# Rows of six experts gathered by quarters of their channels, with a pause of GpSimd behind each tile, and turned by VectorE in squares, in an attention and top-1 mixture-of-experts kernel

## The chip, the cores and the metric

The kernel runs on one core of a Trainium2 chip. Its time is the device time of one execution in microseconds (us). A profile is one execution taken by the hardware profiler; its span is the time from the first to the last instruction seen. The engines are TensorE (PE: matrix products, weight loads shown apart as PEld), VectorE (DVE), ScalarE (ACT), GpSimd (POOL) and SyncE (SP). In this kernel SP issues the plain DMA transfers and POOL the indirect ones, which gather or scatter rows by a list of row numbers.

## The reference

Everything is float32. An attention with 4 batches, 8 heads, 768 positions and 64 channels a head makes a matrix `x` of 3072 tokens by 512 channels. A router sends each token to one of 8 experts, and each expert has two layers.

```python
# attention: a key is seen if it is global (pos < 8) or local (0 <= rel < 96)
scores = q @ k.T / sqrt(D) + bias_of_head_and_distance     # unseen keys: -1e6
attn_out = softmax(scores) @ v
x = attn_out.transpose(0, 2, 1, 3).reshape(3072, 512)
# router
xn, en = x / (norm(x) + 1e-6), expert_emb / (norm(expert_emb) + 1e-6)
logits = xn @ en.T / tau
expert_idx, gate_w = argmax(logits, 1), max(softmax(logits), 1)
# experts: w1 [8, 512, 1024], w2 [8, 1024, 512]
for e in range(8):
    mask = expert_idx == e
    h = maximum(x[mask] @ w1[e], 0)
    out[mask] = gate_w[mask, None] * (h @ w2[e])
```

## The kernel before, in words

**Stages.** The attention and the router come first and take some 200 us. Each token's row of `x` is written to DRAM (`x_dram`), and the list of tokens of each expert is built there. Then the eight experts follow one after the other. In the profile expert 0 stands before 234 us; the first products of experts 1 to 7 begin on PE at 234.2, 268.5, 320.8, 353.6, 390.5, 429.6 and 479.0 us, and the span ends at 522.0. Only experts 2 to 7 are gathered otherwise by the change.

**One expert.** An expert has up to 512 slots, in four tiles of 128 rows. How many of them are computed is read at run time (a `Switch` with one arm for each width, 256 to 512 in steps of 32 from expert 1 on). Its work is:

1. *Gathering* (`gather_rows`, L1000). POOL issues four indirect DMAs, one for each tile; each brings 128 rows of 2 KB to 128 partitions (`xg`, 256 KB). The buffers of `xg` are eight, two experts' worth.
2. *Turning* (`turn_row`). The products need channels on the partitions, tokens along the rows. PE transposes each tile in four pieces of 128x128 (L1026) into PSUM, ACT copies the result in two halves to `xT` (L1029). This is done for expert e+1 while PE works on expert e: one tile behind each of the products 1 to 4 of the first layer (`between`).
3. *First layer* (`first_by_seven`, L1312). The product of `xT` and `w1` is cut in 2x2 blocks and computed with seven block products instead of eight. For this DVE makes sums and differences of the blocks ahead of time: of the tokens (`token_sums`, L1054 to L1057), and of the weights (`first_sums`, L1079 to L1082). DVE adds the products (L1324), ACT takes the relu (L1326, L1343), and the hidden rows lie in `hT`. PSUM has four banks (`big`) for these products.
4. *Second layer.* The tiles from the third on, and the remaining part tile of 64 or 32 rows, are plain products (L1245, L1258) that ACT writes to `y_arm` and `y_part`. The first two tiles are computed as a `Pair`, again with seven products (L1117), whose first is called m. Its results are two tiles `y0` and `y1`, from a pool `yp` of four buffers, so that expert e writes into the buffers of expert e-2. Half of `y0` is written by ACT in `fourth` (L1164); its other half by DVE (L1129) in a function `rest`, which is run after the next expert's first layer.
5. *Scattering* (`scatter_rows`, L1264). POOL issues indirect DMAs that put the rows in the output: two tiles of `y_arm`, two parts, `y0` of the expert before, `y1` of this one; six for each expert, called S(e) here. The first set has seven.

**What sets the order.** A manual schedule: each engine executes its instructions in the order in which the program names them, and semaphores hold an instruction until its data are there. The main loop runs over e = 0 to 7. In each round `prepare(e+1)` issues the four gathers of the next expert, called G(e+1) here; then come the pending scatters S(e-1); then SP is given the loads of `w1` and `w2` of expert e+1; then POOL a `drain` (L1754); then `expert(e)`. So POOL's order is G(0), G(1), drain, G(2), S(0), drain, G(3), S(1), drain, and so on.

**Weights.** `load_weights` issues one DMA of 2 MB for `w1` (L167) and one of 2 MB for `w2` (L168) on SP's queue. Two sets of buffers alternate. The load of expert e+1 waits for product m of expert e-1's pair (`k.out_again`), and that of expert 2 for the last scatter of S(0). The partition p of `w1` holds the channels p, 128 + p, 256 + p and 384 + p.

**Spare time of DVE.** `first_by_seven` and `Pair.begin` take lists of small functions (`spare`). At fixed places between the products they run one list (`fill`), which puts sums for later products into DVE's order there.

Of the kernel before, what the change touches and what calls it, by code (L numbers as in the profile page):

```python
# [9 lines left out]
F32 = mybir.dt.float32  # L10
# [10 lines left out]
P = 128  # L21
# [2 lines left out]
PIECES = 32  # L24
FIRST = 256
LACE = 16
WIDTHS = [128] + list(range(160, CAP + 1, 32))
PAIR = WIDTHS.index(256)

# [134 lines left out]

def load_weights(k, e, w):
    nc = k.nc
    first = nc.sync.dma_start(w[0][:], k.w1[e].rearrange("(c p) f -> p c f", p=P))  # L167
    nc.sync.dma_start(w[1][:], k.w2[e].rearrange("(f p) m -> p f m", p=P))  # L168
    return first

# [824 lines left out]
def gather_rows(k, ids, xgp, NJ=CAP // P, upto=None):  # L995

    xgs, issued = [], []
    for j in range(NJ):
        xg = xgp.tile([P, k.DM], F32, name="xg", tag="xg")
        i = k.nc.gpsimd.indirect_dma_start(  # L1000
            out=xg[:], out_offset=None, in_=k.x_dram[0 : upto or k.N + 1, :],
            in_offset=bass.IndirectOffsetOnAxis(ap=ids[:, j, 0:1], axis=0),
        )
        xgs.append(xg)
        issued.append(i.ins)
    return xgs, issued


def new_turned(k):
    return k.xtp.tile([P, k.NC, 2, CAP // 2], F32, name="xT", tag="xT")  # L1010

# [280 lines left out]
            between(f)  # L1292


def first_by_seven(k, now, hT, w, between, spare):


    nc, h = k.nc, w // 2
    a = first_weights(k, now.w[0])
    b = [[now.xT[:, 2 * i : 2 * i + 2, j] for j in range(2)] for i in range(2)]  # L1300
    s1, s2, s3, s4 = now.first_sums
    t1, t2, t3, t4 = now.token_sums
    out = [[laced(hT[:, 4 * i : 4 * i + 4, 0:w])[:, j] for j in range(2)] for i in range(2)]
    number = [0]

    def banks():
        return [k.big.tile([P, CAP], F32, name="big", tag="big") for _ in range(2)]

    def product(to, x, y, add=False):
        for f in range(4):  # L1310
            for l in range(2):
                nc.tensor.matmul(to[f // 2][:, f % 2 * 256 : f % 2 * 256 + h], lhsT=x[:, l, f * P : (f + 1) * P], rhs=y[:, l, 0:h],  # L1312
                                 start=not (add or f % 2 or l), stop=True, skip_group_check=True)
        between(number[0])
        number[0] += 1

    def pairs(ps, q):
        for i in range(2):
            x = ps[i][:].rearrange("p (f n) -> p f n", f=2)[:, :, 0:h].rearrange("p f (q i) -> p f q i", i=LACE)
            yield x, q[:, 2 * i : 2 * i + 2]  # L1320

    def plus(ps, z, q, last=False):
        for (x, to), (_, z) in zip(pairs(ps, q), pairs(ps, z)):
            nc.vector.tensor_tensor(out=to, in0=x, in1=z, op=ALU.add)  # L1324
            if last:
                nc.scalar.activation(to, to, AF.Relu)  # L1326
        fill()

    def fill():
        for make in spare.pop(0):  # L1330
            make()

    (q11, q12), (q21, q22) = out
    fill()
    x, y = banks(), banks()
    product(x, a[0][0], b[0][0])
    for ps, q in pairs(x, q21):
        nc.scalar.copy(out=q, in_=ps)
    product(y, s2, t2)
    plus(y, q21, q12)  # L1340
    product(x, a[0][1], b[1][0], True)
    for ps, q in pairs(x, q11):
        nc.scalar.activation(q, ps, AF.Relu)  # L1343
    product(y, s3, t3, True)
    plus(y, q21, q22)
    v = banks()
    product(v, s1, t1)
    plus(v, q22, q22, True)
    product(y, a[1][1], t4, True)
    plus(y, q21, q21, True)  # L1350
    product(v, s4, b[1][1], True)
    plus(v, q12, q12, True)


def expert(k, now, coming, widths, unfinished):


    tc = k.tc
    w1, w2 = now.w
    hT = new_hidden(k)  # L1360
    if coming:
        coming.xT = new_turned(k)

    def between(f):
        at = {1: (0,), 2: (1,), 3: (2,), 4: (3,)} if now.e else {5: (0,), 6: (1, 2), 7: (3,)}
        for j in at.get(f, ()) if coming else ():
            turn_row(k, coming.rows, coming.xT, j, k.nc.scalar.copy)

    a = [[hT[:, 4 * j : 4 * j + 4, i * P : (i + 1) * P] for j in range(2)] for i in range(2)]
    now.sums, spare = weight_sums(k, w2)  # L1370
    left, making = hidden_sums(k, a)
    more, ahead = [], []
    if coming:
        coming.token_sums, more = token_sums(k, coming.xT)
        if now.e:
            coming.first_sums, ahead = first_sums(k, coming.w[0])
    spare = [spare[:2], spare[2:], ahead[:1], ahead[1:2], more[:2], []]
    if now.e == 1:
        spare[2:6] = [], ahead[:1], ahead[1:2] + more[:1], more[1:2]
    tiles = range(2 if now.e else 1, CAP // P)  # L1380
    ps = None if now.e else k.work0.tile([P, k.DM], F32, name="work", tag="work")
    k.order = list(range(4, 8)) + list(range(4)) if now.e else list(range(8))
    steps = widths_of(now.e)
    for arm in tc.Switch(now.width.index, len(steps), hint=now.width.hint):
        w = steps[arm]
        if now.e:
            first_by_seven(k, now, hT, w, between, list(spare))
            for make in making:
                make()
        else:  # L1390
            first_by_eight(k, now.xT, w1, hT, w, between)
        for size in (32, 64):
            if w % (2 * size) >= size:
                part_in_arm(k, now, hT, w2, w // (2 * size) * 2 * size, size)
        for j in tiles:
            if j < w // P:
                second_in_arm(k, now, hT, w2, j)
        if ps:
            second(k, ps, hT, w2, range(k.NF // 2))

    def scatters():
        for j in tiles:
            scatter_rows(k, now.y[:, j - 1, :], now.tile_ids[:, j : j + 1])
        for size in (64, 32):
            scatter_rows(k, now.y_part[size][:], now.parts[size][0], P // size)

    def choose_next():
        if coming:
            give_hint(k, coming.e, widths[coming.e])

    out = [scatters]
    if now.e:
        pair = Pair(k, now.rows, a, left, w2, now.sums, not coming)
        choose_next()
        out += unfinished.pop()()
        number = [lambda: widths.append(take_width(k, now.e + 2))] if now.e + 2 < k.E else []
        if now.e == k.E - 2:
            number.append(lambda: load_flag(k))
        if now.e == 2:
            ahead.append(lambda: flag_leftover(k))  # L1420
        pair.begin(spare=(more[2:], number + ahead[2:3], ahead[3:]))
        ps = k.work0.tile([P, k.DM], F32, name="work", tag="work")
        unfinished.append(pair.end(ps[:, 0:256]))
        out.append(pair.scatter(1))
    else:
        choose_next()
        widths.append(take_width(k, 2))
        out += unfinished.pop()()
        for make in more:
            make()  # L1430
        second(k, ps, hT, w2, range(k.NF // 2, k.NF))
        unfinished.append(lambda: end_second(k, now.rows, ps))
    return out
# [172 lines left out]
def kernel(  # L1606
# [40 lines left out]
    with ExitStack() as moe:  # L1647
# [43 lines left out]
        def prepare(e):  # L1691
            t = Net()
            t.e = e
            t.y, t.y_part = ys[e % 2]
            xgs, t.gathers = gather_rows(n, n.ids[:, e], n.xgp)
            t.rows = n.mt[:, e], n.ids[:, e], xgs
            if e < 2:
                t.w = n.w[e]
            else:
                t.w = new_weights(n, (wp_a, n.wp_b)[e % 2])  # L1700
            return t

        with tc.manual_schedule(engines=ORDERED | set(ARMS) | {mybir.EngineType.Pool}):
# [26 lines left out]
            for j in range(CAP // P):  # L1730
                turn_row(n, coming.rows, coming.xT, j, nc.vector.tensor_copy)
            cast(2, n.E)
            split_rows(n, n.mt)
            for y, parts in ys:
                for x in (y, *parts.values()):
# [5 lines left out]
            for e in range(n.E):  # L1741
                now, coming = coming, None
                parts_of(n, now)
                now.width = widths[e]
                if e == 1:
                    now.first_sums = first
                if e + 1 < n.E:
                    coming = prepare(e + 1)
                for scatter in pending:
                    scatter()  # L1750
                if e and coming:
                    wait_for(n, load_weights(n, e + 1, coming.w), [n.outs[-1] if e == 1 else n.out_again])

                nc.gpsimd.drain()  # L1754
                pending = expert(n, now, coming, widths, unfinished)
# [33 lines left out]
```

## Time and profile before

| | |
|---|---|
| time, median of 3 runs | 520.47 us (517.8 to 521.45) |
| profiled execution | 523.85 us, its span 522.0 us |
| busy in the span: PE, DVE, ACT, POOL | 500.9, 301.3, 197.4, 148.7 us |
| lengths of experts 1 to 7 on PE | 34.3, 52.3, 32.8, 36.9, 39.1, 49.4, 43.0 us |
| PE busy in them | 33.0, 52.2, 32.8, 36.6, 39.1, 49.4, 37.6 us |
| DVE busy in them | 22.0, 23.3, 21.4, 21.9, 22.2, 23.2, 16.2 us |
| POOL busy in them | 11.6, 10.6, 11.2, 11.3, 10.9, 6.7, 6.9 us |
| first gather of G(2) to G(7) starts at | 215.8, 238.2, 270.2, 323.9, 356.4, 393.3 us |
| product m of experts 1 to 7 starts at | 254.9, 308.3, 341.5, 377.7, 417.3, 466.7, 504.1 us |
| issue of w1 for experts 2 to 7 | 236.9, 256.9, 310.4, 343.5, 380.3, 419.4 us |

A line of instructions gives the start, the duration, the engine, the line of the code, the operation, what it writes and reads, and in brackets how long the engine had been idle before it and which instruction ended that. A line of the chain gives the start, the duration and what ran. A line of windows gives the stretch, its length, the busy time of PE, PEld, DVE, ACT and POOL with the number of instructions, the granted clock of PE, the mean busy share of the DMA engines, and GB/s.

### The profile page before, as it was taken

To read this page: it belongs to the slowest core of one execution; us is meant where nothing else is said; L and a number is where in the kernel's file an instruction comes from. 1 tells how busy PE (TensorE), PEld (TensorE's weight loads), DVE (VectorE), ACT (ScalarE), POOL (GpSimd) and SP (SyncE) were. 2 spreads that over 40 slices of the span, in tenths; PEclk is the share of its full clock that TensorE was granted. 3 is DMA by queue.
4 is the path that set the end of the run, shared out by engine and by line. 5 is a ranking of instruction groups with operands and counts; after the bars stand their busy time and mean duration, and the time that the engine had idled before them with its cause. 6 is when DMAs were issued, how large, how long until landed. Compare 5 with 4: busy or idle time off the path is not lost.

```text
span 522.0 us, 13698 instructions
## 1 busy us (share of the span) xinstructions
PE 500.9 (96%) x5606; PEld 412.8 (79%) x5606; DVE 301.3 (58%) x602; ACT 197.4 (38%) x493; POOL 148.7 (28%) x169
## 2 busy tenths in 40 slices
PE   8999999999987998899989999999999999999995
PEld 7777787787765687859878659989889789859964
DVE  5646667766774664846745606765646644715531
ACT  4966776777644311303222312412312222302210
POOL 4221121432443326253340024153053050013023
PEclk9999999999998999999999999999999999999999
DMA  8989999998524336818682018457066065001001
GB/s 166 202 174 182 220 238 217 222 232 204 131 69 121 104 62 143 251 46 290 207 287 99 2 50 285 156 198 263 3 217 242 4 224 164 1 15 68 0 22 67
DMA packets 111421, 76.32 MB, mean 146 GB/s; under 512 B 87077, under 2 KB 95269, under 8 KB 111281
## 3 DMA queue, kind: packets, MB, share of 16 engines
q1 hardware_dynamic: 102769, 59.00, 42.6%
q0 software_dynamic: 6912, 15.26, 8.7%
q8 instruction: 63, 1.03, 0.9%
q14 instruction: 77, 0.63, 0.5%
q10 hardware_dynamic: 1600, 0.39, 0.3%
HBM read 61.66 MB, written 17.16 MB: 151 GB/s over the span
## 4 chain that ended last, share of the span: by engine, by line
PE 64%; issue 24%; POOL 5%; DVE 3%; ACT 2%; POOLq 1%; DMA 1%; DVEq 0%
PE big L1312 15%; PE big L1117 8%; PE od L512 7%; PE pa L483 6%; PE pa L458 4%; PE work L1258 3%; PE od L522 3%; PE pa L681 3%; PE work L1117 3%; POOL out_dram L1264 3%; PE work L1245 3%; PE work L1026 2%; PE big L1288 2%; PE pa L585 2%; PE work L1036 1%
## 5 line engine op out<-in xcount | busy, mean ns | idle before, releaser
L496 DVE TENSOR_TENSOR ex<-ex,table 126x768 f32<-126x768 f32 x64 | 60.3, 947 | 41.4 <-ACT ex L489 38.5
L1324 DVE TENSOR_TENSOR hT<-big,hT 128x320 f32<-128x320 f32 (+4 forms) x70 | 39.4, 566 | 49.2 <-PE big L1312 46.8
L1264 POOL DMA_INDIRECT out_dram<-y_arm,tids x17 | 17.0, 1002 | 170.4 <-ACT y_arm L1247 121.3
L489 ACT ACTIVATE ex<-pa 126x384 f32<-126x384 f32 (+1 forms) x128 | 53.7, 476 | 24.0 <-PE pa L483 17.7
L1312 PE MATMUL big<-xT,w1t 128*128 128x160 f32 (+4 forms) x336 | 59.4, 330 | 1.3 <-issue 1.3
L1312 PEld LDWEIGHTS big<-xT,w1t 128*128 128x128 f32 x336 | 54.2, 190 | 4.0 <-issue 2.2
L512 PE MATMUL od<-ex,v 126*64 126x192 f32 (+1 forms) x576 | 46.8, 309 | 0.0
L1000 POOL DMA_INDIRECT xg<-x_dram,idss x32 | 32.3, 1011 | 43.9 <-PE big L1312 21.7
L483 PE MATMUL pa<-qT,kT 64*32 64x128 f32 (+3 forms) x2048 | 40.8, 268 | 2.8 <-issue 2.5
L483 PEld LDWEIGHTS pa<-qT,kT 64*32 64x32 f32 (+1 forms) x2048 | 30.5, 107 | 15.2 <-issue 10.6
L512 PEld LDWEIGHTS od<-ex,v 126*64 126x64 f32 x576 | 35.2, 138 | 7.7 <-issue 3.5
L259 POOL DMA_INDIRECT meta<-mt,slot x24 | 27.4, 1141 | 43.8 <-DVE rd L556 17.8
L1312 PE MATMUL big<-xsum,fsum 128*128 128x160 f32 (+4 forms) x224 | 39.6, 330 | 0.0
L1029 ACT COPY xT<-work 128x256 f32<-128x256 f32 x56 | 18.0, 377 | 56.7 <-PE work L1026 55.3
L1312 PEld LDWEIGHTS big<-xsum,fsum 128*128 128x128 f32 x224 | 36.1, 190 | 1.1
L1245 PE MATMUL work<-w2t,hT 128*128 128x512 f32 x80 | 35.1, 593 | 0.0
L1117 PE MATMUL big<-wsum,hsum 128*128 128x256 f32 x136 | 31.1, 380 | 1.5 <-issue 1.0
L1326 ACT ACTIVATE hT<-hT 128x320 f32<-128x320 f32 (+4 forms) x42 | 21.6, 533 | 25.5 <-DVE hT L1324 25.3
L433 POOL COPY v<-v 30x896 f32<-30x896 f32 (+1 forms) x15 | 16.6, 1119 | 49.0 <-DMA v<-in_v_dram 30.5
L1117 PEld LDWEIGHTS big<-wsum,hsum 128*128 128x128 f32 x136 | 25.7, 190 | 6.0 <-issue 1.8
L1245 PEld LDWEIGHTS work<-w2t,hT 128*128 128x128 f32 x80 | 15.1, 190 | 17.7 <-issue 17.6
L1122 DVE TENSOR_TENSOR ptmp<-big,ptmp 128x256 f32<-128x256 f32 x16 | 6.7, 421 | 37.6 <-PE big L1117 16.9
(246 smaller groups left out, 903.0 us busy)
## 6 DMA issues: line engine op xcount, KB each, us to landing
w1t<-in_moe_w_dram SPq DMA_DIRECT2D x6, 2048.0 KB
w2t<-in_moe_w_dram SPq DMA_DIRECT2D x6, 2048.0 KB
v<-in_v_dram SPq DMA_DIRECT2D x32, 192.0 KB
x_dram<-xs SPq DMA_DIRECT2D x23, 256.0 KB
k<-in_k_dram SPq DMA_DIRECT2D x28, 192.0 KB
q<-in_q_dram SPq DMA_DIRECT2D x28, 192.0 KB
w1t<-in_moe_w_dram SPq DMA_DIRECT2D x32, 128.0 KB
w2t<-in_moe_w_dram SPq DMA_DIRECT2D x32, 128.0 KB
```

The costliest lines, as they stand in the source:

```text
L259: i = nc.gpsimd.indirect_dma_start(out=k.meta[:], out_offset=bass.IndirectOffsetOnAxis(ap=slot[:, t : t + 1], axis=0), in_=mt[:, t, :], in ...
L483: i = nc.tensor.matmul(u.sp[e][k0:k1, a * n + c0 : a * n + c1], lhsT=t.kT[rows, j, k0:k1], rhs=t.qT[rows, j * BLK + c0 : j * BLK + c1], st ...
L489: nc.scalar.activation(u.ex[:, e], u.sp[e][0:ROWS, 0 : 2 * u.n].rearrange("p (a c) -> p a c", a=2), AF.Exp, scale=k.scale)
L496: nc.vector.tensor_tensor(out=exv, in0=exv, in1=tab[:, :, 0 : u.n // BLK, :], op=ALU.mult)
L512: nc.tensor.matmul(g.od[a][e * D : (e + 1) * D, at : at + c1 - c0], lhsT=g.v[0:ROWS, 2 * a + e, u.j, :], rhs=u.ex[:, e, a, c0:c1], start=f ...
L1000: i = k.nc.gpsimd.indirect_dma_start(out=xg[:], out_offset=None, in_=k.x_dram[0 : upto or k.N + 1, :], in_offset=bass.IndirectOffsetOnAxis ...
L1117: i = self.k.nc.tensor.matmul(ps, lhsT=x[:, f, :], rhs=w[:, f, :], start=f == 0 and not add, stop=True, skip_group_check=True)
L1245: nc.tensor.matmul(ps[:], lhsT=hT[:, f, j * P : (j + 1) * P], rhs=w2[:, f, :], start=i == 0, stop=i == k.NF - 1)
L1264: i = k.nc.gpsimd.indirect_dma_start(out=k.out.rearrange("t (i m) -> (t i) m", i=n), out_offset=bass.IndirectOffsetOnAxis(ap=ids, axis=0), ...
L1312: nc.tensor.matmul(to[f // 2][:, f % 2 * 256 : f % 2 * 256 + h], lhsT=x[:, l, f * P : (f + 1) * P], rhs=y[:, l, 0:h], start=not (add or f ...
L1324: nc.vector.tensor_tensor(out=to, in0=x, in1=z, op=ALU.add)
L1326: nc.scalar.activation(to, to, AF.Relu)
```

## The change

For experts 2 to 7, the channels of a row are taken as four quarters of 128. A tile of 128 slots is gathered with four indirect DMAs instead of one: DMA g brings, to each of the 128 partitions, a quarter of a row (512 bytes) into columns 128g to 128g + 127 of `xg`. The lists of row numbers (`squares`, made once by 16 small DVE operations) are mixed so that partitions 32b to 32b + 31 of `xg` hold the quarter b of the tokens in slots 32g to 32g + 31. After that, a transposition that only works inside squares of 32x32 is enough to get channels on partitions: one DVE instruction for each tile (`turn_squares`), which writes to `xT` directly. The transposes on PE and the copies on ACT are gone for these experts. The four turns of expert e+1 stand in DVE's order behind `rest` of expert e and ahead of the pair's first addition.

Behind the four gathers of each tile, POOL executes a small copy that reads the first element of each quarter. It waits until all four have landed, and whatever comes later on POOL stands behind it.

In the turned rows, partition 32b + j and group c hold channel 128b + 32c + j. So `w1` has to be loaded in that order, which is done with four DMAs of 32 partitions (512 KB each) instead of one of 128. Expert 0 and 1 keep their gathers, their turning on PE, and weights loaded earlier in small parts.

Expert 2's four tiles are split: two are gathered before S(0), two after it. The sums of tokens of the next expert, of which two stood inside the first layer, now all stand behind the turns. The sums of weights are spread otherwise over the lists in the first layer.

```diff
@@ load_weights
-    first = nc.sync.dma_start(w[0][:], k.w1[e].rearrange("(c p) f -> p c f", p=P))
+    first = [nc.sync.dma_start(w[0][b * SQ : (b + 1) * SQ], k.w1[e, b * P : (b + 1) * P].rearrange("(c j) f -> j c f", j=SQ))
+             for b in range(4)][0]
@@
+def square_rows(k):
+    k.landed = k.tp.tile([P, 4], F32, name="landed")
+    k.squares = k.tp.tile([P, k.E, CAP // P, 4], I32, name="squares")
+    for b in range(4):
+        for g in range(4):
+            k.nc.vector.tensor_scalar(out=k.squares[b * SQ : (b + 1) * SQ, 2:, :, g], in0=k.mt[g * SQ : (g + 1) * SQ, 2:, :, 0],
+                                      scalar1=4.0, scalar2=float(b), op0=ALU.mult, op1=ALU.add)
+
+def gather_quarters(k, ids, xgs, lo, hi):
+    src = k.x_dram[:, :].rearrange("t (b c) -> (t b) c", b=4)
+    for j in range(lo, hi):
+        for g in range(4):
+            k.nc.gpsimd.indirect_dma_start(
+                out=xgs[j][:, g * P : (g + 1) * P], out_offset=None, in_=src,
+                in_offset=bass.IndirectOffsetOnAxis(ap=ids[:, j, g : g + 1], axis=0),
+            )
+        k.nc.gpsimd.tensor_copy(out=k.landed[0:1, :], in_=xgs[j][0:1, ::P])
+
+def turn_squares(k, xgs, xT, j):
+    half = P // 2
+    k.nc.vector.transpose(
+        out=xT[:, :, :, j * half : (j + 1) * half].rearrange("p c a (g i) -> p g c a i", i=LACE),
+        in_=xgs[j][:].rearrange("p (g c r) -> p g c r", g=4, r=SQ),
+    )
@@ first_by_seven, product
-        between(number[0])
-        number[0] += 1
@@ expert
-        at = {1: (0,), 2: (1,), 3: (2,), 4: (3,)} if now.e else {5: (0,), 6: (1, 2), 7: (3,)}
-        for j in at.get(f, ()) if coming else ():
+        for j in {5: (0,), 6: (1, 2), 7: (3,)}.get(f, ()):
             turn_row(k, coming.rows, coming.xT, j, k.nc.scalar.copy)
...
+            turns = [lambda j=j: turn_squares(k, coming.rows[2], coming.xT, j) for j in range(CAP // P)]
-    spare = [spare[:2], spare[2:], ahead[:1], ahead[1:2], more[:2], []]
-    if now.e == 1:
-        spare[2:6] = [], ahead[:1], ahead[1:2] + more[:1], more[1:2]
+    spare = [[], spare[:2], spare[2:3], spare[3:], ahead[:1], ahead[1:2]]
...
-        pair.begin(spare=(more[2:], number + ahead[2:3], ahead[3:]))
+        for make in turns:
+            make()
+        pair.begin(spare=(more, number, ahead[2:]))
@@ prepare
-            xgs, t.gathers = gather_rows(n, n.ids[:, e], n.xgp)
+            if e < 2:
+                xgs, t.gathers = gather_rows(n, n.ids[:, e], n.xgp)
+            else:
+                xgs = [n.xgp.tile([P, n.DM], F32, name="xg", tag="xg") for _ in range(CAP // P)]
+                gather_quarters(n, n.squares[:, e], xgs, 0, 2 if e == 2 else 4)
@@ the main loop
             cast(2, n.E)
+            square_rows(n)
             split_rows(n, n.mt)
...
                 for scatter in pending:
                     scatter()
+                if e == 1:
+                    gather_quarters(n, n.squares[:, 2], coming.rows[2], 2, 4)
                 if e and coming:
                     wait_for(n, load_weights(n, e + 1, coming.w), [n.outs[-1] if e == 1 else n.out_again])
```

More of the change, by code (lines that the diff above doesn't have):

```diff
@@ L26 @@
 LACE = 16
+SQ = 32
 WIDTHS = [128] + list(range(160, CAP + 1, 32))
@@ L1292, in first_by_eight, with first_by_seven @@
             between(f)
-def first_by_seven(k, now, hT, w, between, spare):
+def first_by_seven(k, now, hT, w, spare):
     nc, h = k.nc, w // 2
@@ L1303, in first_by_seven @@
     out = [[laced(hT[:, 4 * i : 4 * i + 4, 0:w])[:, j] for j in range(2)] for i in range(2)]
-    number = [0]
     def banks():
@@ L1371, in expert @@
     left, making = hidden_sums(k, a)
-    more, ahead = [], []
+    more, ahead, turns = [], [], []
     if coming:
@@ L1386, in expert @@
         if now.e:
-            first_by_seven(k, now, hT, w, between, list(spare))
+            first_by_seven(k, now, hT, w, list(spare))
             for make in making:
```

## The prediction

> **What bounds the kernel now.** I read the page's busy row first, then the windows by expert, the chain that ended last, and GpSimd's instructions in order of time.
>
> ```profile
> PE 500.9 (96%) x5606; PEld 412.8 (79%) x5606; DVE 301.3 (58%) x602; ACT 197.4 (38%) x493; POOL 148.7 (28%) x169
> ```
>
> PE is busy 96% of the span. Whether that holds in each expert is told by the windows that run from one expert's first product to the next one's (here experts 2, 4 and 5):
>
> ```profile
> 268.50:320.80 52.30, 52.22 (x218) 39.81 (x219) 23.25 (x35) 12.03 (x25) 10.60 (x10) 1.00 0.34 120
> 353.60:390.50 36.90, 36.61 (x283) 32.97 (x282) 21.86 (x31) 10.17 (x25) 11.33 (x10) 1.00 0.47 164
> 390.50:429.60 39.10, 39.10 (x202) 33.43 (x200) 22.22 (x31) 10.28 (x24) 10.89 (x10) 1.00 0.45 156
> ```
>
> After the length come PE, PEld, DVE, ACT and POOL. PE fills every stretch. DVE works 22 of about 37 us, POOL 11. So what leaves PE's stream shortens the span one for one, as long as nothing else becomes late. The chain shows what the turning costs on PE (inside expert 3):
>
> ```profile
> 320.97 4.35 PE big L1312 x32
> 325.32 0.44 PE work L1026 x4
> 325.76 2.18 PE big L1312 x16
> 327.93 0.44 PE work L1026 x4
> ```
>
> Four transposes take 0.44 us of the chain between two products. Their row of the groups says 273 ns each, but there they overlap one another, so 0.44 is what is saved. Last, POOL around expert 3's product m (341.5):
>
> ```profile
> 342.39 1.02 POOL L1264 DMA_INDIRECT out_dram<-y_arm,tids  x1 [13.27 <-ACT y L1260]
> ...
> 351.62 0.98 POOL L1264 DMA_INDIRECT out_dram<-y,idss  x1 [2.15 <-DVE y L1122]
> 356.44 0.99 POOL L1000 DMA_INDIRECT xg<-x_dram,idss  x1 [3.84 <-PE big L1312]
> ```
>
> Before this block POOL had idled 13 us. The 3.84 us between last scatter and next gather is the drain of L1754. POOL is now 10 us of scatters, 4 of drain, 5 of gathers, and then it waits for work.
>
> [...] the small scatters land 1.9 to 3.1 us after their start with no load beside them, a full 256 KB scatter 3.7 to 4.6. [...] in the trace small scatters beside a w1 load land after 5.1 to 6.7 us, full gathers beside w2 after 4.3 to 4.8, and that of G(3) beside both after 7.5. [...] The 2 MB loads over 128 partitions last 7.0 to 8.6 us here; no run shows a load over 32. [...]
>
> **The change part by part.** G(e) is the gathering for expert e, S(e) the scatters of expert e (six). POOL's order stays G(e+1), S(e-1), drain.
>
> *PE.* 16 transposes less per expert that prepares a later one, six experts: 4 x 0.44 = 1.76, x 6 = **-10.6 us** if nothing is late. ACT's 48 copies (L1029) go, off the path.
>
> *DVE.* Four transposes of 128x512 per expert, priced as the nearest row, a 128x512 tensor_tensor of 0.69 us (bounds 0.3 and 1.2): 2.8 us. They stand between `rest` and u2; the token sums (the same in number) follow them. In all 25 of 37 us: hidden, since the next expert's second product wants the last of these sums several us later. If the cover went, up to 2 us per expert. 16 tiny operations at 210 us, some 0.17 each, 2.7 us, before `split_rows`: expert 0's products cover them (bounds 0 and 1). Weight sums begin a slot later: 0, covered.
>
> *SP.* Three more issues, 0.38 each, per load: w2 is put in the queue 1.1 us later, hidden by its several us of slack. Nothing else waits in that queue. A w1 load in quarters I price at 10 us (bounds 7, as now, and 14[...]). w1 of experts 3 to 7 is issued a pair before it is read: hidden at all of these.
>
> *POOL.* One tile is now four gathers and a copy that waits for all four landings. Starts are 1.3 us apart: 3 x 1.3 = 3.9 until the fourth starts, then its landing, then 0.4 for wake and copy (POOL copies of this size take 0.18). For the landing of the last 64 KB I take 3.0 alone (bounds 2.3[...], and 3.8, a full scatter) and 5.2 beside a load (bounds 4.0 and 6.5). So a tile costs 7.3 alone, 9.5 beside a load. Loads run some 18 of the 42 us of an expert with its stall, 43%: mean 8.25, **G = 33 us instead of 5** (bounds 29 and 36.6). With S, 6 x 1.32 = 7.9, and 3.9 of drain the POOL cycle is 45 us, while e3, e4, e5 need 31.0, 35.1, 37.3 on PE. In that order POOL can't keep up; what remains is its head start, from e2 (50.5 us).
>
> *Who waits for POOL.* Behind the pause stand S(e-1) and the drain. `fourth` of expert e (L1164, ACT) writes the y0 buffer of expert e-2 (yp has four), whose scatter is fifth in S(e-1), now behind all of G(e+1). So the buffer is free 4 x 1.32 = 5.3 + landing 4.4 = 9.7 us after G(e+1) ends. Behind `fourth` waits the bank that the next expert's second product writes in its second half, 3.3 us after that expert begins (1.5 products of 2.18); with 0.4 for the ACT operation, expert e+1 can begin, as if undisturbed, at **end of G(e+1) + 6.8**. The turning alone would ask for less: copy, four turns, +4.6.
>
> *The chain of times.* G(2) begins at 215.8 as before; two tiles, 14.6 -> 230.4. S(0) has seven scatters, 9.2 -> 239.6. Its last starts at 238.3 instead of 233.19; w1(2) is issued 3.75 after that start, as before, at 242.1 instead of 236.94, lands at 252, and DVE's first sum on it is wanted at 248.4: **+3.4 us** net for expert 1. Expert 2 starts at 268.5 + 3.4 - 1.8 = 270.1; e3 at 320.7; on PE alone e4 at 351.7, e5 at 386.8, e6 at 424.1. POOL: two tiles of G(2) beside loads, 19.0 -> 258.6; then drain + G: G(3) 295.5; and each next one 7.9 + 3.9 + 33 = 44.8 later: G(4) 340.3, G(5) 385.1. S finds its results ready in each. Expert 4: 347.1, no stall. Expert 5: 385.1 + 6.8 = 391.9 instead of 386.8, **stall 5.1**. G(6) 429.9, expert 6 at 436.7 instead of 391.9 + 37.3 = 429.2, **stall 7.5**. G(7) 474.7, +6.8 = 481.5; PE has e7 at 436.7 + 47.6 = 484.3: no stall in the wide e6. Then 43.0 as before: 527.3.
> Sum: -10.6 + 3.4 + 5.1 + 7.5 = +5.4 against the span of 522.0. The profiled execution took 523.85, the median of the runs is 520.47; I carry the difference over: 520.47 + 5.4 = 525.9, said as **526 us**.
>
> **The rivals.** *POOL keeps up.* The sum of stalls is 12.6 at G = 33, and four Gs stand in the time of expert 6, so it moves 4 us per us of G: no stall is left at G = 29.8, 7.5 us a tile. Then -10.6 + 3.4 = -7.2: **513 us**. For it: landings of 64 KB alone could be 2.3, and gathers of G(4) to G(7) beside w2 landed after 4.3 to 4.8 even at 256 KB. Against: 512-byte pieces beside a load, and G(3)'s 7.5.
> *POOL deeper.* G = 36.6, a tile of 9.15, as when landings are 3.6 and 6.5: 4 x 3.6 = +14.4 on 526, **540 us**; it also stalls e5 and perhaps e7. For it: small scatters at 5.1 to 6.7 beside w1. It decides from 8.0 us per tile, where the loss outweighs the saving (slower than before from G = 31.7).
> *A draw.* G about 31.7, or the saving eaten by w1(2) alone: quarters of w1 that take 14 us make expert 1 4 us later still with POOL keeping up: **517 to 521 us**.
> That the change doesn't do what it says: the 96 transposes leave PE's program for certain; only the cost is open.
>
> **How the numbers follow.** About 1% is what a measurement of this kernel tells from no change: under 515.3 is faster, over 525.7 slower. POOL-bound near 526: 0.34 (522 to 532). Deeper: 0.23. Keeps up: 0.23. Draw: 0.20. The cell at 526 lies on the edge of "slower"; of its 0.34, 0.09 falls within 1%, and of the draw all but 0.06, which fall to faster and slower alike. Faster 0.26, same 0.23, slower 0.51. Range 512.5 to 541: all of the middle cases and the near part of both ends.
>
> **What would show it.** Right: no L1026 between products in the chain; POOL's list with gaps of 3 to 5 us ahead of each small copy, G of 33 us; POOL full from 240 to 475; PE idle, on ACT's `fourth` (hidden under "y"), at the second product of experts 5 and 6. Wrong: tiles of 7 us or less and every window 1.76 us shorter; w1 quarters that land after 14 us; or DVE transposes of over 1.2 us, with PE waiting for token sums at the second product of every expert; or gathers of 512 bytes that slow the loads they meet, so that w2 or w1 is late.

## The result, and the profile after

The changed kernel takes **560.58 us** (median of 4 runs, 555.28 to 562.41) against 519.67 us for the kernel before, measured beside it: ratio 1.0771, interval 1.0687 to 1.0855. It is slower by 41 us; 526 us were forecast, and the range ended at 541. The profiled execution has a span of 559.4 us against 522.0.

The busy row of the page, after:

```profile
PE 497.6 (89%) x5510; PEld 409.1 (73%) x5510; DVE 317.7 (57%) x642; ACT 183.3 (33%) x445; POOL 234.7 (42%) x265
```

PE has its 96 transposes less (5510 instead of 5606 matrix instructions). But it is no longer busy all the time: 89% instead of 96%. The windows by expert, for experts 2, 4 and 5 (length, PE, PEld, DVE, ACT, POOL, then the granted clock of PE):

```profile
276.40:327.10 50.70, 50.58 (x204) 38.00 (x202) 27.10 (x41) 9.76 (x17) 25.33 (x26) 1.00 0.44 120
369.20:417.80 48.60, 36.74 (x265) 32.42 (x264) 23.76 (x35) 7.79 (x17) 25.29 (x26) 0.92 0.45 124
417.80:467.20 49.40, 41.02 (x186) 34.23 (x185) 24.15 (x35) 7.89 (x16) 24.07 (x27) 0.91 0.45 122
```

Expert 2 keeps what the change promises: 50.7 instead of 52.3 us. Experts 4 and 5 need about 49 us each instead of 36.9 and 39.1, and PE stands idle in them. Experts 1 and 3 lose too: 46.3 instead of 34.3, 42.1 instead of 32.8. Experts 6 and 7 are as before within 0.4 us. Lost are 12.0, 9.3, 11.7 and 10.3 us in experts 1, 3, 4 and 5; 4.1 us come back before expert 1 starts (230.1 instead of 234.2), and 2 in experts 2 and 6. The 4.1 us are not shown to be the change's: in `before_w1_spread` below, which has the old gathers and turns, expert 1 starts at 227.9.

The chain (the work that ended last, followed back) ahead of 418 us, around the end of expert 4, has no PE in it at all (these are the lines of its last tile):

```profile
396.69 0.97 POOL xg L1026
...
397.97 0.95 POOL xg L1026
...
399.22 0.95 POOL xg L1026
...
400.47 8.59 DMA xg<-x_dram,squares
...
409.23 0.15 POOL landed L1030
```

The same tile in POOL's own list, with the tile before it, which has no load beside it:

```profile
388.53 0.97 POOL L1026 DMA_INDIRECT xg<-x_dram,squares  x1 [0.16 <-issue]
...
396.01 0.18 POOL L1030 COPY landed<-xg 1x4 f32<-1x4 f32 x1 [1.83 <-DMA xg<-x_dram,squares]
396.69 0.97 POOL L1026 DMA_INDIRECT xg<-x_dram,squares  x1 [0.50 <-issue]
...
400.47 0.95 POOL L1026 DMA_INDIRECT xg<-x_dram,squares  x1 [0.30 <-issue]
409.21 0.18 POOL L1030 COPY landed<-xg 1x4 f32<-1x4 f32 x1 [7.79 <-DMA xg<-x_dram,squares]
410.02 1.03 POOL L1297 DMA_INDIRECT out_dram<-y_arm,tids  x1 [0.64 <-issue]
...
421.62 0.99 POOL L1026 DMA_INDIRECT xg<-x_dram,squares  x1 [3.66 <-issue]
```

The copy of the quiet tile waits 1.83 us, that of the last tile 7.79: `w1` of expert 6 was issued at 396.46 and its four quarters took until 409.4. After it come six scatters without a wait (their results have long been ready) and the drain of 3.66 us. From G(3) on POOL waits for PE no more; it runs its own round of 48.3, 55.4, 49.0 and 49.0 us (first gather of G(3) to G(7): 268.9, 317.2, 372.6, 421.6, 470.6), and the experts follow it.

How they follow is told by VectorE and PE:

```profile
409.18 0.71 DVE L1036 STREAM_TRANSPOSE xT<-xg 128x512 f32<-128x512 f32 x1 [10.75 <-DMA xg<-x_dram,squares]
409.82 0.39 DVE L1155 TENSOR_TENSOR ptmp<-big,ptmp 128x256 f32<-128x256 f32 x1
410.13 0.67 DVE L1087 TENSOR_TENSOR xsum<-xT 128x512 f32<-128x512 f32 x1
...
412.29 0.69 DVE L1090 TENSOR_TENSOR xsum<-xT,xsum 128x512 f32<-128x512 f32 x1
412.90 0.42 DVE L1155 TENSOR_TENSOR ptmp<-big,ptmp 128x256 f32<-128x256 f32 x1
```

```profile
414.27 3.78 PE L1150 MATMUL work<-w2t,hsum 128*128 128x256 f32 x8 [9.21 <-ACT ptmp L1203]
417.84 4.07 PE L1344 MATMUL big<-xT,w1t 128*128 128x192 f32 x16
```

The fourth turn waits 10.75 us for its tile. Behind it stand the pair's first addition, the four sums of tokens and the pair's second addition; from these ACT makes what it must write before PE may run the last product of the pair (9.21 us of waiting). Expert 5 begins 8.45 us after G(5), the gathering for it, is through (409.39). The same distance is found at the ends of experts 3 and 5 (8.44 and 8.46).

Expert 1 loses its time in another way. `w1` of expert 2 is issued at 245.43, since S(0) stands behind two tiles of G(2), and it takes 11.4 us (in the chain). VectorE's first sum on it stands ahead of additions that expert 1 needs:

```profile
260.74 1.55 PE L1291 MATMUL work<-w2t,hT 128*64 128x256 f32 x6 [13.41 <-ACT hT L1356]
```

### The profile page after: what moved, and what is told of

The parts are those of the page before. It is cut to its first block, busy times and chain, and to the rows that moved or that the text cites. A ratio compares the mean times of both kernels' runs of the same rounds, so it can differ in the third digit from the quotient of the medians.

```text
span 559.4 us, 13682 instructions
## 1 busy us (share of the span) xinstructions
PE 497.6 (89%) x5510; PEld 409.1 (73%) x5510; DVE 317.7 (57%) x642; ACT 183.3 (33%) x445; POOL 234.7 (42%) x265
## 4 chain that ended last, share of the span: by engine, by line
PE 45%; issue 17%; DMA 16%; POOL 14%; DVE 3%; ACT 2%; POOLq 1%; SPq 0%; ACTq 0%; DVEq 0%
DMA xg<-x_dram,squares 11%; PE big L1344 9%; POOL xg L1026 8%; PE od L514 6%; PE pa L485 5%; PE big L1150 4%; PE pa L460 4%; POOL out_dram L1297 3%; PE od L524 3%; PE pa L683 2%; DMA w1t<-in_moe_w_dram 2%; PE work L1291 2%; PE pa L587 2%; PE big L1321 2%; PE work L1150 1%
## 5 line engine op out<-in xcount | busy, mean ns | idle before, releaser
L1026 POOL DMA_INDIRECT xg<-x_dram,squares x96 | 105.6, 1100 | 53.2 <-issue 44.9
L498 DVE TENSOR_TENSOR ex<-ex,table 126x768 f32<-126x768 f32 x64 | 61.8, 974 | 37.6 <-ACT ex L491 37.3
L1354 DVE TENSOR_TENSOR hT<-big,hT 128x320 f32<-128x320 f32 (+4 forms) x70 | 39.2, 565 | 69.2 <-PE big L1344 39.1
L1344 PE MATMUL big<-xT,w1t 128*128 128x160 f32 (+4 forms) x336 | 61.6, 338 | 4.1 <-ACT hT L1368 4.0
L1344 PEld LDWEIGHTS big<-xT,w1t 128*128 128x128 f32 x336 | 56.8, 196 | 8.4 <-ACT hT L1368 4.9
L1030 POOL COPY landed<-xg 1x4 f32<-1x4 f32 x24 | 8.8, 365 | 81.6 <-DMA xg<-x_dram,squares 81.6
L1150 PE MATMUL work<-w2t,hsum 128*128 128x256 f32 x56 | 19.0, 498 | 25.6 <-ACT ptmp L1203 25.6
L514 PEld LDWEIGHTS od<-ex,v 126*64 126x64 f32 x576 | 35.2, 138 | 7.8 <-issue 3.5
L485 PE MATMUL pa<-qT,kT 64*32 64x128 f32 (+3 forms) x2048 | 38.1, 270 | 0.2 <-issue 0.2
L1150 PEld LDWEIGHTS work<-w2t,hsum 128*128 128x128 f32 x56 | 13.5, 250 | 29.6 <-ACT ptmp L1203 27.2
L1291 PE MATMUL work<-w2t,hT 128*32 128x128 f32 (+1 forms) x320 | 22.1, 328 | 13.4 <-ACT hT L1356 13.4
L1036 DVE STREAM_TRANSPOSE xT<-xg 128x512 f32<-128x512 f32 x24 | 15.4, 684 | 30.8 <-DMA xg<-x_dram,squares 30.8
```

The costliest lines, as they stand in the source:

```text
L485: i = nc.tensor.matmul(u.sp[e][k0:k1, a * n + c0 : a * n + c1], lhsT=t.kT[rows, j, k0:k1], rhs=t.qT[rows, j * BLK + c0 : j * BLK + c1], st ...
L498: nc.vector.tensor_tensor(out=exv, in0=exv, in1=tab[:, :, 0 : u.n // BLK, :], op=ALU.mult)
L514: nc.tensor.matmul(g.od[a][e * D : (e + 1) * D, at : at + c1 - c0], lhsT=g.v[0:ROWS, 2 * a + e, u.j, :], rhs=u.ex[:, e, a, c0:c1], start=f ...
L1026: k.nc.gpsimd.indirect_dma_start(out=xgs[j][:, g * P : (g + 1) * P], out_offset=None, in_=src, in_offset=bass.IndirectOffsetOnAxis(ap=ids[ ...
L1150: i = self.k.nc.tensor.matmul(ps, lhsT=x[:, f, :], rhs=w[:, f, :], start=f == 0 and not add, stop=True, skip_group_check=True)
L1291: nc.tensor.matmul(ps[i * size : (i + 1) * size, 0:m], lhsT=hT[:, f, base : base + size], rhs=w2[:, f, i * m : (i + 1) * m], start=o == 0, ...
```

## The experiments

The kernels below were measured on six chips, and this turned out to matter: the kernel before takes 518.6 to 519.1 us on three of them, 520.9 to 524.7 on the three others. So each kernel is compared with the kernel before on its own chip, and the verdict on the pause rests on four kernels measured on one chip, which come first. The texts of what was expected name theories by letters: A holds the pause for the cause, C the loading of `w1` in quarters, G the 4 KB runs of the quarters, F and F1 the chip.

**The pause and the quarters of w1, two by two on one chip.** `no_pause` leaves out the small copy (nothing of the output comes from it). `w1_linear` keeps the pause and lets VectorE read its squares at a stride of four, so that partition p holds channels 4p to 4p + 3, and `w1` is again one DMA to 128 partitions, with runs of 16 KB. The fourth kernel has both edits.

```diff
-        k.nc.gpsimd.tensor_copy(out=k.landed[0:1, :], in_=xgs[j][0:1, ::P])      # no_pause
```
```diff
-    first = [nc.sync.dma_start(w[0][b * SQ : (b + 1) * SQ], k.w1[e, b * P : (b + 1) * P].rearrange("(c j) f -> j c f", j=SQ))
-             for b in range(4)][0]
+    first = nc.sync.dma_start(w[0][:], k.w1[e].rearrange("(p c) f -> p c f", p=P))
...
-        in_=xgs[j][:].rearrange("p (g c r) -> p g c r", g=4, r=SQ),
+        in_=xgs[j][:].rearrange("p (g r c) -> p g c r", g=4, r=SQ),
```

> The changed kernel once more, so that the four kernels of pause or not and w1 in quarters or in one load stand on one chip. Theory F1 (without a pause the chip decides how long PE stands still beside gathers; with it GpSimd's round is the bound on any chip): 552 to 565.

> As no_pause. Theory F1: 555 to 575 on a chip where the kernel before takes 520.5 or more, 515 to 525 where it takes less. Theory C (w1 in quarters by 4 KB runs makes it slow wherever it runs): 555 or more.

> As w1_linear. Theory F1 and theory A (GpSimd's round of 45 us and more is the bound): 540 to 552 on any chip.

> As w1_linear_no_pause. Theory F1: 511 to 516 where the kernel before takes less than 520, 540 or more where it takes more. Theory C: 511 to 516 on any chip.

Measured, beside 518.70 us for the kernel before:

| | w1 in quarters | w1 in one DMA |
|---|---|---|
| with the pause | 557.49 (1.0779, 1.0696 to 1.0863) | 547.80 (1.0566, 1.0469 to 1.0663) |
| without | 517.43 (0.9980, 0.9957 to 1.0003) | 513.69 (0.9902, 0.9872 to 0.9932) |

The pause costs 40 us with the quarters and 34 without (the four runs of the 547.80 lie between 542.7 and 553.4, so rather 30 to 34). The quarters cost 10 us with the pause and 4 without, net of VectorE's slower reading that takes their place (a transposition took 1079 ns in the fourth kernel, 684 in the changed one). So on this chip the pause is the loss, all of it: without the pause the change is level with the kernel before (the interval holds 1), and without the quarters as well it is 1% below it. Theory F1 and theory A give all four cells; theory C falls with `no_pause` at 517. The windows of `no_pause` on this chip, experts 4 and 5:

```profile
350.70:385.90 35.20, 34.80 (x266) 31.27 (x266) 24.77 (x37) 7.90 (x17) 22.08 (x21) 1.00 0.63 166
385.90:424.60 38.70, 37.60 (x185) 31.75 (x184) 24.09 (x35) 8.01 (x16) 24.97 (x26) 1.00 0.61 161
```

PE is full again, in 35.2 and 38.7 us, while POOL does the same gathers. Its list (the first and the last three of one G; the first scatter behind them):

```profile
364.81 1.24 POOL L1026 DMA_INDIRECT xg<-x_dram,squares  x1 [7.33 <-issue]
366.36 0.98 POOL L1026 DMA_INDIRECT xg<-x_dram,squares  x1 [0.30 <-issue]
...
385.18 0.95 POOL L1026 DMA_INDIRECT xg<-x_dram,squares  x1 [0.30 <-issue]
386.44 0.95 POOL L1026 DMA_INDIRECT xg<-x_dram,squares  x1 [0.30 <-issue]
387.69 1.02 POOL L1296 DMA_INDIRECT out_dram<-y_arm,tids  x1 [0.30 <-issue]
```

Sixteen gathers take 22.9 us, not 37. Of the 10.6 us that the transposes took from PE, `no_pause` gives back 4 in expert 1, where PE still waits 5.22 us for the late `w1` (38.2 us instead of 34.3); experts 2 to 6 are 5.6 us shorter in sum, not 8.8. In the kernel with both edits PE waits 2.18 us in expert 1.

**One pause instead of four** (the copy behind the loop over the tiles, on the last tile).

```diff
-        k.nc.gpsimd.tensor_copy(out=k.landed[0:1, :], in_=xgs[j][0:1, ::P])
+    k.nc.gpsimd.tensor_copy(out=k.landed[0:1, :], in_=xgs[hi - 1][0:1, ::P])
```

> w1_linear with one small copy behind all four tiles instead of one behind each. Theory A (a pause costs what the last landing takes, 3 us alone and 5 to 7 beside a load, four times an expert, and GpSimd's round of 45 us is the bound): G 21 + 3 to 6, a round of 36 to 39 us against 31 to 37 on PE; 515 to 523 us. Theory A'' (any wait of GpSimd for a gather holds up the rest): 535 us or more.

514.82 us, 0.9937 (0.9915 to 0.9958). A wait of POOL for a gather is harmless in itself:

```profile
355.48 0.18 POOL L1029 COPY landed<-xg 1x4 f32<-1x4 f32 x1 [5.16 <-DMA xg<-x_dram,squares]
```

It waits 5.16 us here, beside a load, and nobody is late for it: PE has no gap over 1.1 us from there to expert 7. Only the sum of four in a round longer than the expert makes the loss. Theory A holds.

**The turns later.** The fourth kernel of the table, with the turns behind the pair's first addition and the sums of tokens behind its second.

```diff
-        for make in turns:
-            make()
-        pair.begin(spare=(more, number, ahead[2:]))
+        pair.begin(spare=(turns, more + number, ahead[2:]))
```

> w1_linear_no_pause with VectorE's four turns behind the pair's first addition and the four sums of tokens behind its second, instead of both ahead of the pair's first and second. If the gaps of 1 to 2 us on PE inside the pair come from the additions that stand behind 4.3 us of turns, they go: 508 to 512 us. If not (the sums come too late for the next expert's second product): 514 to 520 us.

513.60 us, 0.9906 (0.9869 to 0.9942), against 513.89 and 513.69 for the kernel that it was made from, on other chips. That is no gain that the measurement tells: of the gaps in the pair the one of expert 3 goes, that of expert 1 stays (2.8 us), and one of 1.6 us appears between two products of expert 3's first layer. The expectation of 508 to 512 was a miss.

**A chip that is worse for this.** Four kernels were measured on it: `no_pause`, `w1_linear`'s forerunner `w1_wide` with and without pause, and the kernel before with `w1` in quarters.

> The changed kernel without the small copies behind each tile; quarters, squares and w1 in quarters stay. Theory A (the pause makes GpSimd the bound, a round of G 37 + S 8 + drain 4 = 49 us against 31 to 37 us that an expert needs on PE): sixteen gathers at 1.3 us are 21 us, a round 33 us, PE is the bound again except perhaps in expert 3; w1(2) still comes some 3 us late; 512 to 518 us. Theory B (not the pause, but gathers of 512-byte pieces beside w1 in quarters, which land late, so that VectorE's turns are late anyway): over 540 us, with VectorE idle for some 8 us ahead of a turn.

560.80 us, 1.0740 (1.0667 to 1.0814): taken alone it says the opposite of the table above, that the pause costs nothing. With `before_w1_quarters` below it led to theory C, that the quarters keep everything else waiting.

```diff
-    first = nc.sync.dma_start(w[0][:], k.w1[e].rearrange("(c p) f -> p c f", p=P))
+    first = [nc.sync.dma_start(w[0][b * 32 : (b + 1) * 32], k.w1[e].rearrange("(c p) f -> p c f", p=P)[b * 32 : (b + 1) * 32])
+             for b in range(4)][0]
```

> The kernel before with w1 in four DMAs of 32 partitions each, its own layout kept. Theory A: w1 takes 11.5 to 12 us instead of 7 to 8.6, hidden everywhere but for expert 2, whose first sum wants w1 at 247 us and gets it at 249 to 250: +2 to +4, 522 to 525 us. Theory B (the slow load is a main cost by itself): over 532 us.

> before_w1_quarters once more, on another chip if there is one. Theory F1 (on a chip where the kernel before takes less than 520 a slow load only costs what is late for it): w1(2) lands 3 us late, 520 to 525. Theory C (the quarters keep the next arm's instructions waiting anywhere): 531 to 536.

533.64 us, 1.0247 (1.0175 to 1.0319), and on another chip 538.74, 1.0307 (1.0235 to 1.0380), with the kernel before at 520.91 and 524.65. The quarters take 11.2 to 12.2 us in the first of these traces instead of 7.0 to 8.6. Beyond the late `w1` of expert 2, a second delay is longer than before: PE's jump into the next expert's arm (these lines are of the second trace).

```profile
L1785 PEldq COMPARE_BRANCH  x16: 292/348/7277, 207.7 to 509.4; - x16
```
```profile
274.53 2.04 PE L1313 MATMUL big<-xT,w1t 128*128 128x256 f32 x4 [5.15 <-issue]
```

The longest jump lasts 7.28 us (3.76 in the kernel before); it starts at 266.8 and ends just before expert 2, ahead of which PE idles 5.15 us with nothing that the profile shows as awaited. Both were measured on chips on which the kernel before takes over 520 us, so what the quarters cost the kernel before on the others is not measured; the table's 4 us is the nearest.

The cut over every fourth partition, with the same counts and sizes:

```diff
+    first = [nc.sync.dma_start(w[0][b::4], k.w1[e].rearrange("(c p) f -> p c f", p=P)[b::4])
+             for b in range(4)][0]
```

> The kernel before with w1 in four DMAs of 32 partitions, but every fourth partition (b, b+4, ...) instead of 32 neighbours; counts, sizes and bytes as in before_w1_quarters. Theory C ([...]the load lasts 12 us, and the instructions of the next arm and w1(2) come behind it): loads last 7 to 8.6 us again and the time is that of the kernel before, 519 to 523. Theory D (four DMAs instead of one, or more semaphores and queue work, make it): loads last 11 us or more, 530 to 536.

518.97 us, 1.0007 (0.9993 to 1.0022). Its loads last 7.4 to 9.0 us, and a packet of 4 KB takes 0.16 us, in the quarters of 32 neighbours 0.32. So it is the neighbours that make the load slow, not the number of DMAs: on that, theory C holds (with quarters of neighbours the loads last 11 to 14 us on all five chips on which they were traced). What the slow load costs in time is not told by this pair, since the two ran on different chips.

`w1_wide` cut `w1` by its second index, each DMA over 128 partitions:

```diff
+    first = [nc.sync.dma_start(w[0][:, c], k.w1[e].rearrange("(b c j) f -> c b j f", c=4, j=SQ)[c])
+             for c in range(4)][0]
```

> The changed kernel, pause kept, w1 in four DMAs of 512 KB cut by the other index, so that each goes to all 128 partitions (same 4 KB rows, same place of every element). Theory A[...]: w1 lands in 7 to 8.6 us, that tile falls to 8 to 10 us, G from 37 to 32 to 33, the stall of expert 1 from 13.4 to 4 to 8 us; 527 to 538 us. Theory B (the 4 KB packets in front of the small ones make it, whatever the partitions): the tile stays at 12 to 13 us and only the stall of expert 1 shrinks; 548 to 556 us.

> Both: no small copies, and w1 in four DMAs over all 128 partitions. Theory A: nothing is late but perhaps w1(2) by 1 us, the transposes are gone from PE: 509 to 514 us, under the kernel before. Theory B (small gathers cost by themselves, or VectorE gets too late with the turns): 520 us or more.

580.84 us (1.1106, 1.1008 to 1.1204) and 578.49 (1.1067, 1.0980 to 1.1154). They don't test what they were made for, whether the tile beside `w1` gets shorter when each DMA goes to all partitions: the loads took 24 to 31 us, with the time of 3 to 4 packets running at once instead of 11 to 14. Why is not shown; nothing is concluded from the two runs but that this cut is bad.

**The edits of the table on a second chip**, with the kernel before at 519.07 us:

> The changed kernel, pause kept, with VectorE's squares read at stride four, so that partition p holds channels 4p to 4p+3 and w1 is one DMA over 128 partitions. Theory C (w1 in quarters holds up the tile beside it, the fetches of instructions and w1(2)): w1 lands in 7 to 9 us, the tile beside it takes 8 to 9.5 us instead of 13, G 33 instead of 37 to 44, the stall of expert 1 falls from 13.4 to 5 to 9 us, GpSimd's round is 45 us: 525 to 538. Theory A' (the pause alone is the bound, whatever the load): 550 to 560.

> The same without the small copies. Theory C1 (the 560 us without the pause came from w1 in quarters in front of the instruction fetches): nothing is late, 510 to 518. Theory C2 (sixteen gathers in a row without a pause keep the fetches waiting by themselves, as PE's gaps of 1 to 2 us in expert 0 of no_pause say, where no weight load runs): expert 0 stays 6 to 8 us later than before, and PE has gaps with no wait in most experts; 525 to 545.

546.39 us (1.0517, 1.0491 to 1.0544) and 513.89 us (0.9886, 0.9834 to 0.9937). The first lies 8 us above what theory C gave it: `w1` lands in 6.5 to 7.8 us now, but the tile beside it still takes 9.3 to 12.3 us. The second is theory C1's.

**Is it the neighbours or the chip?** `w1_linear_no_pause` with `w1` in quarters of 32 neighbours again:

```diff
-    first = nc.sync.dma_start(w[0][:], k.w1[e].rearrange("(p c) f -> p c f", p=P))
+    first = [nc.sync.dma_start(w[0][b * SQ : (b + 1) * SQ], k.w1[e].rearrange("(p c) f -> p c f", p=P)[b * SQ : (b + 1) * SQ])
+             for b in range(4)][0]
```

> w1_linear_no_pause with its w1 cut in four DMAs of 32 neighbouring partitions again (16 KB runs, same places). Theory C[...]: loads of 11 to 13 us, 550 to 563 us. Theory E (the 4 KB runs or the slower squares make the difference): 512 to 525 us.

519.26 us, 1.0019 (0.9992 to 1.0046), with loads of 11.4 to 13.1 us. Theory C had 550 and more. The same kernel again, with `no_pause`, and a third with its runs cut to 4 KB (sixteen DMAs), on one chip:

```diff
+    first = [nc.sync.dma_start(w[0][b * SQ : (b + 1) * SQ, c], k.w1[e].rearrange("(p c) f -> p c f", p=P)[b * SQ : (b + 1) * SQ, c])
+             for b in range(4) for c in range(4)][0]
```

> no_pause once more, in one call and on one chip with the next two. Theory C (w1 in quarters of 32 neighbours by 4 KB runs costs it): 555 to 563 again. Theory F (what was seen belonged to that chip): 512 to 530.

> linear_quarters_no_pause once more beside it. Both theories: 515 to 523; it is the partner for the comparison on one chip.

> linear_quarters_no_pause with each quarter of w1 cut in four DMAs more, so that each run of a partition is 4 KB instead of 16 KB (sixteen DMAs of 128 KB; layout and VectorE's reading stay). Theory G[...]: 545 to 563 us. Theory H (it is the place of the rows or the squares' reading order in no_pause that costs): 516 to 526 us.

573.87 (1.0945, 1.0825 to 1.1065), 570.57 (1.0882, 1.0786 to 1.0978) and 580.38 us (1.0986, 1.0865 to 1.1107); the kernel before took 524.01. The very kernel that took 519.26 takes 570.57 on this chip, and the 4 KB runs are no different within the intervals. That fells theory C and theory G: without the pause it is the chip that decides, or something else that differs between the measurements, for each chip was used once. What PE does there is seen at the same place of expert 3, on this chip:

```profile
364.93 1.89 PE L1149 MATMUL big<-w2t,hT 128*128 128x256 f32 x8
376.11 3.78 PE L1149 MATMUL work<-w2t,hsum 128*128 128x256 f32 x8 [9.29 <-issue]
```

and on the other:

```profile
344.08 1.89 PE L1149 MATMUL big<-w2t,hT 128*128 128x256 f32 x8
347.64 1.99 PE L1149 MATMUL work<-w2t,hsum 128*128 128x256 f32 x8 [1.67 <-ACT ptmp L1202]
```

PE idles 9.29 us here, for which the profile names no cause, where the other chip has 1.67 us and names ACT's copy L1202. The same copy, on this chip and on the other:

```profile
375.58 0.47 ACT L1202 ACTIVATE ptmp<-work,mts 128x256 f32<-128x256 f32 x1 [7.25 <-remote]
```
```profile
347.13 0.46 ACT L1202 ACTIVATE ptmp<-work,mts 128x256 f32<-128x256 f32 x1
```

PE goes on within 0.1 us of this copy on both. So PE waits for ACT, and ACT had idled 7.25 us. The copy reads a PE product whose record ends at 365.1, but the signal of PE right behind which it starts stands in the trace at 375.56, 10.5 us later. In six such places, in the traces of the three kernels on this chip and of `no_pause` on the earlier one, that signal comes 8 to 15 us behind the record (some signals are missing from these traces); on the other chip it comes at once. VectorE's four turns were done at 364.4, so late gathers are not the cause here. The packets of the loads take as long on both (median 1.27 and 1.26 us for 16 KB). Why PE's product, or its signal, is late there no run has settled. That stays open, as does what the changed kernel and the one without pause and quarters would take on such a chip.

## Why the prediction was wrong, point by point

**The bound was right, the price was not.** The prediction said that GpSimd can't keep its order any longer, that the pauses make its round longer than the experts, and that PE then stalls around the starts of experts 5 and 6. The table shows the pause as the cause (34 to 40 us). Expert 4 stalls too, which was not forecast.

**The step that failed: the price of a tile, and with it G = 33.** From G(3) to G(6) a tile beside no `w1` took 8.13 us from its first gather to that of the next tile, or for the last to the end of its copy (mean of 11; 7.3 were priced), one beside `w1` 12.94 (mean of 5; 9.5 were priced). G came to 36.6, 43.6, 36.8 and 37.1.

- The landing in quiet was right: 2.5 to 3.8 us after the fourth gather (once 4.4), priced 3.0. What was short is the issue: a gather lasts up to 1.9 instead of 0.95 us now and then (three intervals of 4.4 us in the mean, not 3.9), and the copy with the next start takes 0.7 to 1.2, not 0.4.
- The landing beside `w1` was outside its own upper bound: 7.5 to 9.6 us, priced 5.2, bounded by 6.5. The prediction had taken that bound from 2 MB loads over 128 partitions, and had priced the slow quarters only for who waits for `w1`, not for the gather that lands beside them. In all five cases POOL's copy starts within 2.2 us of the load's last packet. So what such a tile costs seems to be what is left of the load when its fourth gather starts. With one load over all partitions (`w1_linear`) the same wait is 5.3 to 7.9 us, so most of it is there without the quarters and their longer load makes the rest.
- Beside `w2` it depends on the same thing. The tiles that began in a `w2` load at 372.6 and 421.6 took 7.6 and 7.5 us, but their fourth gather started 1.4 and 1.3 us before that load ended. In `w1_linear` the tiles of 269.0 and 319.3, whose fourth gather had 4.8 and 5.7 us of `w2` ahead, took 11.0 and 11.1. The prediction's reading that gathers beside `w2` landed after 4.3 to 4.8 us was too low: by the last of their signals in that trace it was 4.8 to 6.8.
- 5 of these 16 tiles met `w1`, less than the 43% that were let meet a load. At 43% the measured prices would give G = 40.8; the mean was 38.5. So one mistake hid, by luck, a part of the other.

G(3) to G(6) are 22 us longer in sum than forecast, each added to expert 6's start just as the sensitivity of 4 us per us of G had it.

**The rest of POOL's round was right.** S and drain took 11.8 us (360.8 to 372.6) as forecast.

**G(2), S(0) and w1(2).** S(0)'s last scatter began at 241.76, not 238.3: the second tile took 9.0 us, and three scatters 1.6 to 2.0. The issue followed 3.7 us later, as forecast; the quarters landed after 11.4 us, near the priced 10, which was the author's estimate between the 7 us of a load in the trace of before and twice that. But VectorE wanted them at 244 us, not at 248.4, since expert 1 had begun 4.1 us earlier in this execution. So PE stood still for 13.4 us there, where 3.4 was forecast. It costs little in the end: from expert 3 on POOL's round sets the times. G(3) began at 268.9 instead of 262.5, and it is these 6.4 us that stay.

**Who waits for POOL.** The forecast named ACT's `fourth` behind the scatter of `y0`, at +6.8, and gave the turning alone +4.6. It was the turning, at +8.45, and PE waited at the last product of the pair, not at the next expert's second product. The missed part is what stands behind the last turn: in VectorE's order the pair's additions (409.82 and 412.90 us at the end of expert 4) and the four token sums between them come behind it (409.18), and PE's last product of the same pair (414.27) comes behind these. Of the 8.45 us 1.9 are this product itself at half its pace (3.78 us, 1.89 in the kernel before), which the forecast had at nothing. That added 1.65 us once, for POOL runs free.

**The sum.** 527.3 of span were forecast. 6.4 (G(2)) + 22.4 (four Gs and 0.3 of S and drain) + 1.65 (the way from POOL to PE) = 30.5 us later for expert 6, which begins at 467.2 instead of 436.7; experts 6 and 7 add 1.4 and 0.2. That gives 559.4.

**What was priced right.** VectorE's transposition took 684 ns, priced 0.69 from the nearest row. No transpose is left between products. A slow `w1` for experts 3 to 7 is hidden, as forecast: in `no_pause` on the table's chip PE has no gap over 1.1 us from expert 2 on.

**The rivals.** "POOL deeper" was the outcome, with its decision point: a tile over 8.0 us. It had G = 36.6 and 540 us, since its landing beside `w1` stopped at 6.5 (its bounds of 3.8 and 6.5 give 37.0; measured were 38.5 in the mean, and the late G(2) came on top). "POOL keeps up" is what the kernel does without the pause: 517.43 against 518.70 us is -1.3 where -7.2 was worked out, and without the quarters, whose 3.4 us then fall away, 513.69 is -5.0 where -10.6 would follow. So the saving itself is about half of what was priced; what takes the rest no run separates.

## What to carry to other kernels

Price an in-order queue by its whole round, with every wait in it, and set that beside the time that the bounding engine needs for the same round; near equality, a mistake of 1 us per wait is multiplied by waits and rounds, and the range has to follow that product. A transfer that is made slower must be priced twice: for those who read it, and for whatever lands beside it (here a gather: 2.5 to 3.8 us in quiet, 7.5 to 9.6 beside the quarters). When a comparison across chips surprises, measure both kernels on one chip before building on it; here one kernel took 519 and 571 us on two chips between which the kernel before differed by 1%.

## What had not been expected of the hardware

- A load of `w1` in four DMAs to 32 neighbouring partitions each takes 11 to 14 us for 2 MB, and a 4 KB packet 0.32 us instead of 0.16. Every fourth partition instead gives 7.4 to 9.0 us and 0.16. Why neighbours are slower no run shows.
- VectorE's 128x512 transposition took 684 ns when it reads rows of 32 neighbours, and 1075 ns at a stride of four elements (`w1_linear`).
- After an idle of 9.2 us, eight matrix instructions of PE took 3.78 us instead of 1.89, and the next sixteen 4.07, those after them 2.76. The granted clock of experts 1, 3, 4 and 5 is 0.85 to 0.92, where it was 1.00. So that stall cost PE some 3 us more than its length; where POOL sets the pace, as here, only what stands ahead of the next expert counts. In this trace the clock fell to half 2.4 to 5.4 us after PE had stopped, in its four stalls of 7.5 to 13.4 us. The forecast had left this out of its stalls of 5.1 and 7.5 us.
- Without the four pauses, the chips fall in two kinds: 514 to 519 us on three, 561 to 580 on two, where PE idles up to 13.6 us at a time; in the places read above ACT's copy ahead of it is late too. The cause is not known.
